# Four whole-unit buffers for the normalized attention output, and an earlier place for the chain of unit 3

## The chip, the cores and the metric

The kernel runs on one core of a Trainium2 chip. What counts is the device time of one launch, in microseconds. Three runs of the kernel before took 279.30, 278.63 and 280.29 us, a median of 279.3. The profiled execution of it took 279.81 us.

A core has five engines that run side by side and wait for each other through semaphores: PE (TensorE, matrix products into PSUM), DVE (VectorE), ACT (ScalarE), POOL (GpSimd) and SP (SyncE). POOL issues the loads here, SP issues the stores and the transposing DMAs.

## The reference

```
q, k, v: (8, 8, 576, 64)            # batch, heads, sequence, head_dim
per batch and head, in 9 chunks of 64 rows:
    attn = softmax(q_c @ k_c.T / 8)
    out  = attn @ v_c
x = out, heads side by side: (4608 tokens, 512)
h = x @ w_in                         # (512, 2048)
g = h * sigmoid(beta * h)            # beta: one value for each of the 2048 columns
result = g @ w_out                   # (2048, 512) -> (4608, 512), float32
```

## The kernel before

The 4608 tokens are cut into 18 units of 256 tokens. Two units make a block of 512, so there are 9 blocks, numbered j = 0 to 8. All products run in float16 with float32 sums in PSUM.

**Attention of a unit u** is a chain over four engines.

- `emit_T(u)` brings q and k into the layout that PE needs: two transposes on DVE (L161) for units below 9, two transposing DMAs on SP (L156) from unit 9 on. At its end `loads_to(u + 4)` lets POOL issue the loads of a later unit (L103, L109, L117). The q and k tiles have 4 buffers, so a load waits for the transpose of the unit four before.
- `emit_sc(u)` computes the scores on PE (L229, or L216 from unit 9 on) and their exponential on ACT (`et`, L238 or L222). With `split=True` the exponential is done in two halves.
- `emit_pv(u)` multiplies with v on PE (L267, or L253 from unit 8 on). v has an extra column of constant value, so that the row sum comes out beside the result.
- `emit_norm(u, s)` divides half s of the unit (128 tokens) by the row sum and writes `x16` in float16: a reciprocal (L302) and a product (L306) on DVE. From unit 8 on, `emit_norm_whole` does this with two reciprocals (L285, L287), two products on DVE (L275) and two small ones on ACT (L286).
- The transposed tile `xt` comes from `x16` in one of three ways: `emit_xt_pe(u, s)` by PE (L322) and a copy on ACT (L326); `emit_xt_unit(2)` the same for both halves at once (L334, L337); `emit_xt_dma(u, s)` by a transposing DMA on SP (L341), from unit 6 on.

The tiles `x16` come from the pool `x_p`. Units 0 to 7 take one tile of 1 KB per partition for each half, tag `x16`, 4 buffers. Units 8 to 17 take one tile of 2 KB for the whole unit, tag `x32`, 2 buffers. A buffer is free again when the PE transposes or the DMAs that read it are done.

**The first layer of a block**: `emit_m(j, m, c0, n)` computes 128 of the 2048 hidden columns, for n tokens (512, or 256 when a unit comes alone), with four matmuls (L365) into `hps`; ACT applies a tanh (`sg`, L377); DVE makes the gated value `gt` (`emit_mg`, L353). With `gate=False` the gate is not issued there but by a later `emit_mg`.

**The second layer.** For block 0 `emit_t(0, t, k0, k1)` multiplies row group t with rows k0 to k1 of w_out, four matmuls of 128x512 in a call (L390), into the PSUM tile `ops` of that row group. There are 16 calls: s = 0 to 3 outside, t = 0 to 3 inside. The last call for each t also copies the tile on ACT (L400) and stores it from SP (L402). The other blocks use seven products of smaller matrices in place of eight (`emit_prod`, L582), with sums of gates (`emit_sum`, L429) and differences of weights (`emit_wt`, L420).

**PSUM.** `hps`, `ops`, `xp` of `emit_xt_pe`, and the accumulators of block 1 share one pool with 4 buffers (`ps_p`, tag "p"). From unit 8 on, `emit_pv` takes two buffers of that pool (`xe`) beside its own tile in `ps_s`; the scores of the next unit take that same tile's place in `ps_s`.

**Order.** The order on every engine is the order in which the program emits the instructions (`tc.manual_schedule()`). Up to and with the first half of block 1 it is written out by hand. From there on a list of items with due times is sorted for each block; an item that is due earlier is emitted earlier. The hand-written part that matters is the second layer of block 0, with the attention of units 2 and 3 between its calls, and then the first eight `emit_m(1, ...)` on unit 2 alone, with the end of the chain of unit 3 between them:

```
sc(3)  m0 m1 m2(gate later)  pv(3)  norm(3,0) gate2  m3(gate later)  norm(3,1) gate3
m4  xt_pe(3,0)  m5  m6  xt_pe(3,1)  m7
```

After these come `emit_m(1, 0..7)` on the tokens of unit 3, from the sorted list.

Of the kernel before, what the change touches and what calls it, by code (L numbers as in the profile page):

```python
# [9 lines left out]
FP16 = mybir.dt.float16  # L10
# [5 lines left out]
def kernel(  # L16
# [11 lines left out]
    B, H, S, D = q.shape  # L28
# [4 lines left out]
    KFF = DFF // 128  # L33
# [112 lines left out]
    qT = {}  # L146
    kT = {}
# [131 lines left out]
    def emit_norm_whole(u, s):  # L279
        x, y = x_t[u][0:2]  # L280
        if s == 0:
            rx = rd_p.tile([128, 2, 8, 1], FP32, tag="rx", name="rx")
            x16 = x_p.tile([128, 2, 2, 4, D], FP16, tag="x32", name="x16", bufs=2)
            for r in range(2):
                nc.vector.reciprocal(out=rx[:, r, 7], in_=y[r][:, D:D + 1])  # L285
                nc.scalar.activation(out=x16[:, 1, r, 3], in_=y[r][:, 0:D], func=ACTF.Copy, scale=rx[:, r, 7])  # L286
            nc.vector.reciprocal(out=rx[:, :, 0:7], in_=x[:, :, :, D:D + 1])  # L287
            norm_part(x16[:, 0], x[:, :, 0:4], rx[:, :, 0:4])
            x_t[u] = (x, rx, x16)
            x16_t[u, 0] = x16[:, 0]  # L290
            return
        x, rx, x16 = x_t.pop(u)
        norm_part(x16[:, 1, :, 0:3], x[:, :, 4:7], rx[:, :, 4:7])
        x16_t[u, 1] = x16[:, 1]

    def emit_norm(u, s):
        if u >= WV:
            emit_norm_whole(u, s)
            return
        x = x_t.pop((u, s))  # L300
        rd = rd_p.tile([128, 2, 4, 1], FP32, tag="rd", name="rd")
        nc.vector.reciprocal(out=rd, in_=x[:, :, :, D:D + 1])  # L302
        x16 = x_p.tile([128, 2, 4, D], FP16, tag="x16", name="x16")
        for r in ([0, 1] if u < 2 else [slice(0, 2)]):
            o = x16[:, r]
            nc.vector.tensor_tensor(  # L306
                out=o, in0=x[:, r, :, 0:D], in1=rd[:, r].to_broadcast(list(o.shape)), op=ALU.mult
            )
        x16_t[u, s] = x16
# [101 lines left out]
    def emit_wt(i, qs=(0, 1)):  # L411
        for q in qs:
            o = [t[:, 4 * q:4 * q + 4, :] for t in wt]
            a, b = {
                0: (w_half(0, q, 1), w_half(0, q, 0)),
                1: (w_half(1, q, 1), o[0]),
                2: (w_half(1, q, 1), w_half(0, q, 1)),
                3: (w_half(1, q, 0), o[1]),
            }[i]
            nc.vector.tensor_tensor(out=o[i], in0=a, in1=b, op=ALU.subtract)  # L420
# [10 lines left out]
    def emit_beta():  # L431

        nc.vector.tensor_tensor(out=rb, in0=bt, in1=bt, op=ALU.mult)
        nc.vector.tensor_scalar(out=rb, in0=rb, scalar1=1e-20, scalar2=None, op0=ALU.is_lt)
        nc.vector.scalar_tensor_tensor(out=rb, in0=rb, scalar=2e-10, in1=bt, op0=ALU.mult, op1=ALU.add)
        nc.vector.tensor_scalar(out=bs, in0=rb, scalar1=2.0, scalar2=None, op0=ALU.mult)
        nc.vector.reciprocal(out=rb, in_=rb)
# [173 lines left out]
    with tc.manual_schedule():  # L611
# [62 lines left out]
            emit_m(0, m)  # L674
        for s in range(4):
            for t in range(4):
                if s == 2 and t == 1:
                    emit_T(2)
                    for i in (0, 2, 1, 3):
                        emit_wt(i, (0,))  # L680
                    emit_wt(0, (1,))
                if s == 2 and t == 2:
                    emit_sc(2)
                if s == 3 and t == 0:
                    emit_pv(2)
                    emit_norm(2, 0)
                    emit_norm(2, 1)
                    emit_T(3)
                if s == 3 and t == 3:
                    emit_xt_unit(2)  # L690
                emit_t(0, t, 4 * s, 4 * s + 4)
        emit_beta()
        emit_sc(3, True)
        for m in range(2):
            emit_m(1, m, 0, 256)
        emit_m(1, 2, 0, 256, gate=False)
        emit_pv(3)
        emit_norm(3, 0)
        emit_mg(1, 2)
        emit_m(1, 3, 0, 256, gate=False)  # L700
        emit_norm(3, 1)
        emit_mg(1, 3)
        emit_m(1, 4, 0, 256)
        emit_xt_pe(3, 0)
        emit_m(1, 5, 0, 256)
        emit_m(1, 6, 0, 256)
        emit_xt_pe(3, 1)
        emit_m(1, 7, 0, 256)

        def att_items(u, a0, w):  # L710
# [19 lines left out]
        for j in range(1, NB):  # L730
# [12 lines left out]
            items = []  # L743
            if j == 1:
                items += [(0.04 * m, 0, ("h", m)) for m in range(8)]
                items += [(0.32 + 0.085 * (m - 8), 0, ("m", m)) for m in range(8, KFF)]
                items += [(0.30, 3, ("T", 4)), (0.52, 2, ("sc", 4)), (0.70, 2, ("pv", 4)), (0.71, 3, ("norm", 4, 0)),
                          (0.80, 3, ("norm", 4, 1)), (0.56, 3, ("Th", 5, "kT")), (0.63, 3, ("Th", 5, "qT"))]
                items += [(c, 3, ("wt", i)) for i, c in ((1, 0.47),)]
            else:  # L750
                m0 = {2: 0.36, 4: 0.09}.get(j, 0.02)
                if j < QB:
                    items += [(m0 + (1 - m0) * m / KFF, 0, ("m", m)) for m in range(KFF)]
                else:
                    lane = LANE[2 if j == QB else j == NB - 1]
                    cost = [1 if it[0] == "q" and it[2] == 3 else 2 for it in lane]
                    for n, it in enumerate(lane):
                        c, e, f = (0.98 * sum(cost[:n + d]) / sum(cost) for d in (0, 1, 2))
                        items.append((c, 0, it))
                        if it[0] == "m":  # L760
                            items.append((c + 0.04, 3, ("mg", it[1])))
                        elif it[0] == "last":
                            pass
                        elif it[2] == 2:
                            if j == NB - 1 and it[1] == 3:
                                f = e
                            items += [(f - 0.002, 2, ("qs", it[1], 2)), (f - 0.001, 2, ("qs", it[1], 1)),
                                      (f + 0.03, 3, ("qt", it[1], 0))]
                        elif it[2] == 3:
                            items += [(c + 0.001, 2, ("qs", it[1], 0)), (c + 0.04, 3, ("qt", it[1], 1))]  # L770
                    if j == QB:
                        items.append((0.18, 6, ("open",)))
                        items += [(0.20 + 0.01 * n, 6, ("tx", QB, n)) for n in range(4)]
                        items += [(0.26 + 0.01 * n, 6, ("ws", 2, n)) for n in range(4)]
                        items += [(0.40 + 0.02 * n, 5, ("ws", 3, n)) for n in range(4)]
                        items += [(0.62 + 0.02 * n, 5, ("ws", 1, n)) for n in range(4)]
                    if j + 1 < NB:
                        items += [(0.70 + 0.06 * n, 5, ("tx", j + 1, n)) for n in range(4)]
                for i, p in enumerate((1, 2, 6, 5, 7, 3, 4)):
                    for t in range(2):  # L780
                        w = 1.06 if j == NB - 1 else 0.98
                        items.append(((0.002 if j >= QB else 0) + w * (2 * i + t) / 14, 1, ("prod", p, t)))
                if j == NB - 1:
                    for i, c in ((2, 0.72), (0, 0.80), (1, 0.86)):
                        items.append((c, 4, ("pre", i)))
                for i in range(4):
                    s0 = (0.01, 0.08, 0.25, 0.33)[i] if j == 2 else 0.005 + 0.07 * i
                    if j >= QB:
                        s0 = (0.003, 0.10, 0.33, 0.48)[i]
                    items.append((s0, 4, ("sum", i)))  # L790
                if j == 2:
                    items += [(c, 3, ("wt", i)) for i, c in ((2, 0.36), (3, 0.55))]
                    items += [(0.03, 0, ("sc", 5)), (0.06, 2, ("xp", 4, 0)), (0.09, 2, ("xp", 4, 1)),
                              (0.17, 2, ("pv", 5)), (0.18, 3, ("norm", 5, 0)), (0.19, 3, ("norm", 5, 1)),
                              (0.24, 3, ("T", 6)), (0.53, 3, ("T", 7)), (0.60, 3, ("T", 8)), (0.61, 3, ("T", 9)), (0.80, 3, ("T", 10)),
                              (0.30, 2, ("xp", 5, 0)), (0.32, 2, ("xp", 5, 1))]
                for u, a0, w in ATT.get(j, ()):
                    items += att_items(u, a0, w)
# [87 lines left out]
```

## Time and profile before

| | |
|---|---|
| median of three runs | 279.3 us (278.63 to 280.29) |
| profiled execution: whole time, span of its instructions | 279.81 us, 277.9 us |
| DVE busy | 208.8 us, 75% of the span |
| ACT busy | 165.1 us, 59% |
| POOL busy | 95.4 us, 34% |
| granted TensorE clock | 0.9 or more of full speed in all 40 slices |
| DMA | 36.42 MB, 131 GB/s in the mean; 0.9 busy or more in each of the first 27 of 40 slices |
| transposing DMA of `xt`, issue to landing | 2.4 to 9.0 us, median 6.4 (24 of them) |
| load of a whole unit's k (128 KB), issue to landing | median 11.8 us |

The profile tells for each engine when it was busy, and for each idle stretch which event ended it. "Busy" on PE is modelled and overlaps from one matmul to the next, so the time that a group takes is read from its start to the start of the next group. In a row of a timeline the first number is the start in us from the start of the span, the second the duration, then engine, line, operation, the tiles that are written and read, the shape and the count; in brackets the idle time of the engine before it and what ended it. A row of the list of waits names the waiting engine and line, then what it waited for, then the total, the number of times and the longest, in us.

### The profile page before, as it was taken

The page shows a single profiled execution, that of the slowest core. Times are in us where ns is not written, and L with a number is a line of the kernel's source. Part 1 is how long each engine was busy: PE and PEld are TensorE (multiplying, and loading weights), DVE is VectorE, ACT ScalarE, POOL GpSimd, SP SyncE. Part 2 cuts the span into 40 slices and gives each one's busy share as a digit, 9 for nine tenths or more (in the row PEclk, how much of TensorE's full clock was granted, in tenths as well). Part 3 has the DMA queues.
Part 4 walks back from the last instruction along what each step waited for, and adds up shares of the span by engine and source line. Part 5 has one row for each costly group of instructions (what it writes and reads, how often), then busy time and mean ns, then how long its engine had stood idle before and what let it go on. Part 6 is the DMA issues. An engine that isn't in the chain of part 4 may idle for free.

```text
span 277.9 us, 7779 instructions
## 1 busy us (share of the span) xinstructions
PE 268.0 (96%) x3226; PEld 183.7 (66%) x3226; DVE 208.8 (75%) x391; ACT 165.1 (59%) x295; POOL 95.4 (34%) x122
## 2 busy tenths in 40 slices
PE   8799999899999999999999989999999999999995
PEld 3565446656756566666666656666877887788874
DVE  2567566899988688668865857679997978787961
ACT  3378416886555566556555744667557495858721
POOL 8954478498539843343336310000000000000000
PEclk9999999999999999999999999999999999999999
DMA  9999999999999999999999999973112102110223
GB/s 138 163 195 203 190 180 187 233 173 167 171 130 132 169 166 153 177 142 140 154 150 194 140 155 212 186 133 88 38 41 75 40 0 78 38 40 0 77 78 113
DMA packets 141762, 36.42 MB, mean 131 GB/s; under 512 B 125856, under 2 KB 141216, under 8 KB 141728
## 3 DMA queue, kind: packets, MB, share of 16 engines
q0 software_dynamic: 99136, 18.10, 84.4%
q1 hardware_dynamic: 42592, 17.84, 34.9%
q8 instruction: 25, 0.41, 0.6%
q14 instruction: 9, 0.07, 0.1%
HBM read 36.71 MB, written 9.44 MB: 166 GB/s over the span
## 4 chain that ended last, share of the span: by engine, by line
PE 65%; DVE 13%; DMA 10%; ACT 6%; issue 3%; POOL 2%; SPq 0%; ACTq 0%; DVEq 0%; POOLq 0%
PE hps L365 24%; PE ya L582 12%; PE yb L582 9%; DMA xt<-x 5%; PE acc L582 5%; PE ops L390 4%; PE qx L478 3%; DMA qu<-in_q_dram 3%; ACT hq L510 3%; PE qz L478 3%; DVE gt L353 3%; DVE gt L524 2%; DMA h<-in_k_dram 2%; DVE x L306 2%; PE sc L229 1%
## 5 line engine op out<-in xcount | busy, mean ns | idle before, releaser
L365 PE MATMUL hps<-xt,win 128*128 128x512 f16 (+1 forms) x504 | 110.8, 356 | 1.7 <-ACT xt L326 0.7
L353 DVE SCALAR_TENSOR_TENSOR gt<-sg,hps 128x512 f16<-128x512 f32 (+1 forms) x113 | 68.8, 617 | 32.4 <-ACT sg L377 31.5
L377 ACT ACTIVATE sg<-hps,bt 128x512 f32<-128x512 f32 (+1 forms) x113 | 70.5, 636 | 36.8 <-PE hps L365 36.4
L365 PEld LDWEIGHTS <-win 128*128 128x128 f16 x504 | 47.7, 98 | 35.3 <-issue 2.5
L582 PEld LDWEIGHTS <-sm 128*128 128x128 f16 x512 | 49.4, 98 | 12.5 <-issue 0.3
L582 PEld LDWEIGHTS <-gt 128*128 128x128 f16 x384 | 36.8, 98 | 10.4 <-DVE gt L524 0.6
L117 POOL DMA_DIRECT2D vbig<-in_v_dram x40 | 33.8, 854 | 24.9 <-DMA ku<-in_k_dram 6.3
L582 PE MATMUL ya<-wt,sm 128*128 128x256 f16 x200 | 25.9, 273 | 0.0
L103 POOL DMA_DIRECT2D qu<-in_q_dram x20 | 17.0, 855 | 16.7 <-DVE qT L161 7.1
L103 POOL DMA_DIRECT2D ku<-in_k_dram x20 | 16.9, 857 | 14.7 <-DMA qu<-in_q_dram 7.6
L524 DVE TENSOR_SCALAR gt<-hq,rb 128x512 f16<-128x512 f32 x32 | 14.5, 482 | 7.5 <-ACT hq L510 6.5
L429 DVE TENSOR_TENSOR sm<-gt 128x2048 f16<-128x2048 f16 (+1 forms) x17 | 19.7, 1156 | 0.3
L510 ACT ACTIVATE hq<-hq,bs 128x256 f32<-128x256 f32 (+1 forms) x32 | 17.1, 610 | 1.8 <-DVE hq L503 1.8
L238 ACT ACTIVATE et<-sc 128x1024 f16<-128x1024 f32 (+1 forms) x10 | 8.3, 852 | 12.3 <-PE sc L229 12.3
L275 DVE TENSOR_TENSOR x<-x,rx 128x512 f16<-128x512 f32 (+1 forms) x20 | 11.9, 620 | 4.4 <-DMA xt<-x 4.2
L599 ACT COPY osb<-ya 128x512 f32<-128x512 f32 x18 | 10.6, 589 | 7.6 <-PE ya L582 7.1
L390 PE MATMUL ops<-wout,gt 128*128 128x512 f16 x64 | 14.5, 379 | 0.0
L582 PE MATMUL yb<-wout,gt 128*128 128x256 f16 x104 | 13.9, 273 | 0.2
L478 PEld LDWEIGHTS <-ws 128*128 128x128 f16 x128 | 12.5, 98 | 2.0 <-issue 0.6
L582 PE MATMUL yb<-wt,sm 128*128 128x256 f16 x104 | 13.5, 273 | 0.1
L582 PE MATMUL ya<-wout,gt 128*128 128x256 f16 x104 | 13.5, 273 | 0.0
L582 PE MATMUL yb<-wout,sm 128*128 128x256 f16 x104 | 13.5, 273 | 0.0
(99 smaller groups left out, 347.0 us busy)
## 6 DMA issues: line engine op xcount, KB each, us to landing
out_dram<-osb SPq DMA_DIRECT2D x32, 256.0 KB, 3.5
vbig<-in_v_dram POOLq DMA_DIRECT2D x32, 128.0 KB, 7.2
qu<-in_q_dram POOLq DMA_DIRECT2D x18, 128.0 KB, 7.8
ku<-in_k_dram POOLq DMA_DIRECT2D x18, 128.0 KB, 11.8
win<-in_moe_w_in_dram POOLq DMA_DIRECT2D x8, 256.0 KB, 9.1
wout<-in_moe_w_out_dram POOLq DMA_DIRECT2D x4, 512.0 KB, 12.8
qu<-in_q_dram POOLq DMA_DIRECT2D x5, 256.0 KB, 6.6
ku<-in_k_dram POOLq DMA_DIRECT2D x5, 256.0 KB, 7.2
```

The lines of the kernel that those rows point to most:

```text
L103: nc.gpsimd.dma_start(out=tv[off:off + n, sp], in_=src[b, :, s:s + n, :].rearrange("h p d -> p h d"),)
L117: nc.gpsimd.dma_start(out=vbig[off:off + n, i % NV, :, 0:D], in_=v[b, :, s:s + n, :].rearrange("h p d -> p h d"),)
L275: nc.vector.tensor_tensor(out=x16, in0=x[:, :, :, 0:D], in1=rd.to_broadcast(list(x16.shape)), op=ALU.mult)
L353: nc.vector.scalar_tensor_tensor(out=gt_t[j][:, m, c0:c0 + n], in0=sg[:, 0:n], scalar=1.0, in1=hps[:, 0:n], op0=ALU.add, op1=ALU.mult,)
L365: nc.tensor.matmul(out=hps[:, 0:n], lhsT=w_in16[m // 2][:, kk, (m % 2) * 128:(m % 2) * 128 + 128], rhs=xr[:, c0 // CH:(c0 + n) // CH, 2 * ...
L377: nc.scalar.activation(out=sg[:, 0:n], in_=hps[:, 0:n], func=ACTF.Tanh, scale=bt[:, m:m + 1])
L390: nc.tensor.matmul(out=ops, lhsT=gt_t[j][:, kk, t * 128:(t + 1) * 128], rhs=w_out16[kk // 4][:, kk % 4, :], start=(kk == 0), stop=(kk == K ...
L429: nc.vector.tensor_tensor(out=sm[i][:, lo:hi, :], in0=a, in1=b, op=op)
L478: nc.tensor.matmul(out=dst[:, s, :], lhsT=lhsT, rhs=rhs, start=(p in (1, 2, 5) and s == 0 and kk == 0), stop=(s == 1 and kk == 1), skip_gr ...
L510: nc.scalar.activation(out=o, in_=src, func=ACTF.Silu, scale=bs[:, m:m + 1])
L524: nc.vector.tensor_scalar(out=gt_t[j][:, m, :], in0=hq[:, b].rearrange("p c q -> p (c q)"), scalar1=rb[:, m:m + 1], scalar2=None, op0=ALU. ...
L582: nc.tensor.matmul(out=dst, lhsT=lhsT, rhs=rhs, start=(p in (1, 2, 5) and kk == 0 and (t == 0 or last)), stop=(kk == 7 and (t == 1 or last ...
```

## The change

Two things are changed, in the tile pool and in the hand-written order; no instruction is added or removed.

First, all units take whole-unit tiles `x16` of 2 KB from one tag with the pool's 4 buffers. Units below 8 allocate the tile in `emit_norm(u, 0)` and write its halves. The pool takes the same 8 KB per partition.

Second, in the second layer of block 0 the attention of units 2 and 3 is emitted one call of `emit_t` earlier, and the last call, `emit_t(0, 3, 12, 16)`, is emitted after pv(3). `emit_beta` comes before `emit_T(2)`. T(3) does q before k. The second half of the weight difference `wt[0]` comes after T(3). In the first eight `emit_m(1, ...)`, m 0 and 1 (in place of 2 and 3) have their gates issued later, m 2 has it behind those of m 0 and 1, and `emit_xt_pe(3, 1)` stands before m 6.

```
         if s == 0:
             rx = rd_p.tile([128, 2, 8, 1], FP32, tag="rx", name="rx")
-            x16 = x_p.tile([128, 2, 2, 4, D], FP16, tag="x32", name="x16", bufs=2)
+            x16 = x_p.tile([128, 2, 2, 4, D], FP16, name="x16")
...
+    xw_t = {}
+
     def emit_norm(u, s):
...
-        x16 = x_p.tile([128, 2, 4, D], FP16, tag="x16", name="x16")
+        if s == 0:
+            xw_t[u] = x_p.tile([128, 2, 2, 4, D], FP16, name="x16")
+        x16 = xw_t[u][:, s]
...
         for s in range(4):
             for t in range(4):
-                if s == 2 and t == 1:
+                if s == 2 and t == 0:
+                    emit_beta()
                     emit_T(2)
                     for i in (0, 2, 1, 3):
                         emit_wt(i, (0,))
-                    emit_wt(0, (1,))
-                if s == 2 and t == 2:
+                if s == 2 and t == 1:
                     emit_sc(2)
-                if s == 3 and t == 0:
+                if s == 2 and t == 3:
                     emit_pv(2)
                     emit_norm(2, 0)
                     emit_norm(2, 1)
-                    emit_T(3)
-                if s == 3 and t == 3:
+                    emit_T(3, ("qT", "kT"))
+                    emit_wt(0, (1,))
+                if s == 3 and t == 2:
                     emit_xt_unit(2)
-                emit_t(0, t, 4 * s, 4 * s + 4)
-        emit_beta()
+                if s < 3 or t < 3:
+                    emit_t(0, t, 4 * s, 4 * s + 4)
         emit_sc(3, True)
-        for m in range(2):
-            emit_m(1, m, 0, 256)
-        emit_m(1, 2, 0, 256, gate=False)
+        emit_m(1, 0, 0, 256, gate=False)
+        emit_m(1, 1, 0, 256, gate=False)
         emit_pv(3)
         emit_norm(3, 0)
+        emit_mg(1, 0)
+        emit_t(0, 3, 12, 16)
+        emit_m(1, 2, 0, 256, gate=False)
+        emit_norm(3, 1)
+        emit_mg(1, 1)
         emit_mg(1, 2)
-        emit_m(1, 3, 0, 256, gate=False)
-        emit_norm(3, 1)
-        emit_mg(1, 3)
+        emit_m(1, 3, 0, 256)
         emit_m(1, 4, 0, 256)
         emit_xt_pe(3, 0)
         emit_m(1, 5, 0, 256)
+        emit_xt_pe(3, 1)
         emit_m(1, 6, 0, 256)
-        emit_xt_pe(3, 1)
         emit_m(1, 7, 0, 256)
```

A third edit writes the constant 0.085 as 0.0850 and changes nothing.

More of the change, by code (lines that the diff above doesn't have):

```diff
@@ L745 @@
                 items += [(0.04 * m, 0, ("h", m)) for m in range(8)]
-                items += [(0.32 + 0.085 * (m - 8), 0, ("m", m)) for m in range(8, KFF)]
+                items += [(0.32 + 0.0850 * (m - 8), 0, ("m", m)) for m in range(8, KFF)]
                 items += [(0.30, 3, ("T", 4)), (0.52, 2, ("sc", 4)), (0.70, 2, ("pv", 4)), (0.71, 3, ("norm", 4, 0)),
```

## The prediction

> **What bounds the kernel now.** I read the page's busy times first, then the list of who waited for whom on PE, then the timeline of PE, DVE and ACT around each wait.
>
> ```profile
> PE 268.0 (96%) x3226; PEld 183.7 (66%) x3226; DVE 208.8 (75%) x391; ACT 165.1 (59%) x295; POOL 95.4 (34%) x122
> ```
>
> PE is the bound: about 10 us of the 277.9 us span are not PE, and some 6 of those are the head and the tail. So a gain can only be PE time that is a wait. The list for PE (total, times, longest) has the few that matter here:
>
> ```profile
> PE hps L365 <- ACT xt L326: 0.7, 3, 0.3
> PE hps L365 <- ACT x L286: 0.6, 1, 0.6
> PE xp L322 <- DVE x L306: 0.5, 1, 0.5
> PE sc L216 <- PE hps L365: 0.4, 1, 0.4
> ```
>
> The first and third belong to the chain of unit 3, at 46 to 53 us; the second and fourth to the normalization of unit 14, at 162 to 166 us. PE's timeline of the first place (start, duration, work):
>
> ```profile
> 46.29 0.71 PE L229 MATMUL sc<-qT,kT 32*64 32x64 f16 x64
> 46.94 1.48 PE L365 MATMUL hps<-xt,win 128*128 128x256 f16 x12
> 48.35 0.45 PE L267 MATMUL x<-vbig,et 64*64 64x65 f16 x32
> 48.73 1.05 PE L365 MATMUL hps<-xt,win 128*128 128x256 f16 x8
> 50.24 0.40 PE L322 MATMUL xp<-ident,x 128*128 128x128 f16 x4 [0.46 <-DVE x L306]
> 50.56 0.60 PE L365 MATMUL hps<-xt,win 128*128 128x256 f16 x4
> 51.31 0.60 PE L365 MATMUL hps<-xt,win 128*128 128x256 f16 x4 [0.15 <-ACT xt L326]
> 51.74 0.39 PE L322 MATMUL xp<-ident,x 128*128 128x128 f16 x4
> 52.06 0.60 PE L365 MATMUL hps<-xt,win 128*128 128x256 f16 x4
> 52.94 6.24 PE L365 MATMUL hps<-xt,win 128*128 128x256 f16 x44 [0.28 <-ACT xt L326]
> ```
>
> Durations overlap, so I count from start to start. Twelve 256-wide matmuls take 48.35 - 46.94 = 1.41 us with a 0.11 us change of shape, so one m (four of them) is 0.43. Then 48.73 to 50.24 is 1.51 for two m (0.87): 0.64 lost. 50.56 to 51.31 is 0.75 for one: 0.32 lost. 52.06 to 52.94 is 0.88 for one: 0.45 lost. Together 1.4 us. Why the transpose at 50.24 was late is in DVE's and ACT's timelines:
>
> ```profile
> 48.55 0.78 DVE L353 SCALAR_TENSOR_TENSOR gt<-sg,hps 128x256 f16<-128x256 f32 x2 [1.31 <-ACT sg L377]
> 49.25 0.20 DVE L302 RECIPROCAL rd<-x 128x8 f32<-128x8 f32 x1
> 49.49 0.69 DVE L306 TENSOR_TENSOR x<-x,rd 128x512 f16<-128x512 f32 x1
> ```
> ```profile
> 47.07 1.09 ACT L238 ACTIVATE et<-sc 128x512 f16<-128x512 f32 x2
> ```
>
> The gates of m 0 and 1 stand before the normalization on DVE, and they waited for ACT, which did the exponentials until 48.16. The second place (all engines, cut to its rows):
>
> ```profile
> 161.70 1.04 PE L582 MATMUL yb<-wout,gt 128*128 128x256 f16 x8
> 162.94 0.52 ACT L286 ACTIVATE x<-xe,rx 128x64 f16<-128x64 f32 x2 [3.43 <-DMA xt<-x]
> 162.95 0.69 DVE L275 TENSOR_TENSOR x<-x,rx 128x512 f16<-128x512 f32 x1 [2.44 <-DMA xt<-x]
> 163.30 1.02 PE L365 MATMUL hps<-xt,win 128*128 128x512 f16 x4 [0.56 <-ACT x L286]
> ```
>
> Unit 14 takes the buffer of unit 12 (two buffers), whose transposing DMA was issued by SP only at 155.67 and landed at 162.83 in the chain of waits. ACT and DVE stand still, a PSUM bank stays taken, and PE runs out: 161.70 to 163.30 is 1.60 for 0.87 of work, 0.73 lost. The next scores (165.03 to 166.46) need the bank that DVE releases with its second product at 165.81: 1.43 for 0.87 and a usual 0.1, so 0.46 lost. Together 1.2 us.
>
> **The four buffers.** No instruction is added: the same products write into halves of one tile. Unit 14 now takes unit 10's buffer, whose DMA was issued at 131.61 and, at the longest landing of this kind (9.0 us), was done by 141. ACT's turn then is right after its reciprocal (160.29 + 0.23), and PE wants the bank at 162.57: 2 us of cover. The waits of units 13 and 15 go too, but PE felt neither. Gain: 1.2 us; bounds 0.7 (only the first gap closes) and 1.2 (both).
>
> **The chain of unit 3.** One group (four 128x512, 8.73 us for ten groups between 30.71 and 39.44, so 0.87) moves from before the scores to behind the PV product, so sc(3) starts at 46.29 - 0.87 = 45.42, and sc(2) at 38.57, pv(2) at 41.04. What each needs:
> - T(2) still waits for the load of ku (35.77) and ends at 37.08: 1.5 us before sc(2), where 2.4 were.
> - norm(2) moves with pv(2) and ends at 43.2. T(3) follows, q first: qT 43.1, kT 43.7 to 44.4. POOL's wait that ended at 43.07 on a ku landing tells that unit 3's k is in by 43.0: 0.7 us before kT and 1.7 before it would hold sc(3).
> - beta's five DVE operations (45.20 to 47.24) go before T(2), where DVE sat idle 3.45 us; the subtraction wt(0), 0.6 us, goes behind T(3), where DVE has nothing until the reciprocal at 47.4. Both cost nothing; without that cover 2.0 and 0.6 us of DVE.
> - The store of the last row group leaves SP about 2 us later; the next store on SP is at 71.83. POOL's loads for unit 7 wait for T(3), but also for a DMA lane until 57.37: unmoved.
>
> A sentence apart: the Trainium skill, "SBUF — State Buffer", on the shared port pair, says that a VectorE operation with two SBUF inputs can shut GpSimd's reads out for its whole length, and by that (an estimate, if issuing reads through it) the moved subtraction could hold POOL's loads for up to 0.65 us; the time would stay 277.2, since the loads it would meet, of unit 5, are not used before 61 us. Here POOL issued two loads in 1.40 us at 37.51 while such subtractions ran, no slower than its mean of 0.85 for one.
>
> Now the walk, by the durations above. m 0 and 1 from 46.07; ACT's exponentials end at 48.16 - 0.87 = 47.29, so the second half of pv(3), due at 47.24, waits about 0.1. The kept group runs 47.55 to 48.42, m 2 to 48.85. DVE meanwhile does reciprocal 47.43 (0.38 after the product's start, as at 41.91 and 42.29), product 47.67 to 48.36, gate 0 to 48.68, the second half to 49.53, gate 1 to 49.86, gate 2 to 50.26. m 3 takes m 0's bank: 48.85, on time. m 4 takes the kept group's bank, which ACT has copied at 48.42 + 0.2 + 0.59 = 49.2: on time at 49.28. The transpose of half 0 takes m 1's bank: 49.9, 0.2 late. m 5 needs gate 2: 50.3. Half 1 at 50.73, m 6 at 51.08 (ACT's xt copy ends at 51.03), m 7 to 51.94, and the next m needs the second xt copy: 52.0 against 52.94. Gain 0.9 us. Bounds: 1.4 if every loss goes; below nothing, -0.4, if DVE's and ACT's queues, now with one PSUM bank less for a while, stop PE twice more by 0.64, the longest stop of this stretch. I take the walk.
>
> Another sentence apart: the Trainium skill, "TensorE: Matmul & The Clock Gate", on a second failure mode, says that short idles between groups from cycling PSUM banks can make the clock drop to half; by it the 5 us of matmuls in this stretch, which with one bank held idles in just this way, could take twice as long, and the sum would be about 282 us (an estimate from that page). Here the granted clock is 1.00 from 45 to 60 us with those very idles in it.
>
> **Sum.** 0.9 + 1.2 = 2.1 us: the span goes to 275.8. The profiled run took 279.81, 1.9 us beyond its span and 0.5 over the median of 279.3; off the median that is **277.2 us**. What is earlier on PE must not be late on a DMA. Closest is the first m of block 3 at 98.16: its xt came from a DMA issued at 90.67, and by the median landing of 6.4 it was in at 97.1. PE would want it at 97.3, and its DMA is issued 0.9 earlier as well. Scores of unit 16 (176.1) have their transposed q, issued until 165.75, by about 171.5.
>
> **Rivals.**
> - *Only one part pays.* Loads keep DMA busy in nearly every tenth up to 190 us, and transposes land after 2.4 to 9.0 us. If the landing of block 3 stays or slips by 0.9, the first gain is handed back at 98 us, and 1.2 stays: 278.1. If instead the chain gains and the 162 us wait returns as another wait there, 0.9 stays: 278.4. For: the narrow 0.2 us at 97. Against: PE never waited for a DMA in this trace.
> - *Slower: unit 3's k comes late.* T(3) sits one group earlier, in DVE's strict order, before the wt subtraction and norm(3). From a landing at 44.7 on, PE loses each microsecond, at 46.8 both gains are gone, and at 48.2 the kernel is slower by over 0.5%. A ku issued at 34.91 with the median landing of its kind (11.8) comes at 46.7, and with 13.8 (the median of the q loads of 64 KB) at 48.7: 277.2 + 4.0 = 281.2. Against: it came by 43.0 here, and the loads ahead of it don't move.
> - *It does more.* All 1.4 goes in the chain and the 0.42 us before the scores at 65.86 as well: 276.3.
>
> **Chances.** The forecast 0.68 (its own range 276.4 to 278.0), one part 0.20, slower 0.07, more 0.05. The three runs before spread over 0.6%, so about 0.5%, 1.4 us, is what a measurement can tell from no change; that line is at 277.9. Faster: 0.9 of the first, all of the last and a quarter of the second, 0.71, cut to 0.68 for the margin of only 0.7 us; same 0.25; slower 0.07. Range: 276.3 (the third rival) to 278.9 (one part, with 0.5 of scatter).
>
> **What would show it.** PE's timeline between sc(3) and the next block of m's: 6.6 us with the kept group in it (6.65 without, before); no 0.46 idle ahead of the first xp; sc(3) near 45.4. No wait of ACT L286 or L275 on DMA xt, and m after m at 162 us without a gap. It is wrong if kT for unit 3 waits for ku, if the m's after pv(3) wait 0.5 us or more on gates, or if an hps near 97 us waits for xt.

## The result and the profile after

The kernel after takes 278.08 us (median of 9 runs, 277.3 to 278.34) and the kernel before 279.3 us (9 runs, 278.63 to 280.29): a ratio of 0.9953, 95% interval [0.9936, 0.9971], or 1.3 us less (0.8 to 1.8; the medians differ by 1.2). The interval does not reach 1, so the kernel is faster, but by just under the half per cent that the prediction drew as its line. A second measurement gave 0.9946 [0.9932, 0.996]. The forecast was 2.1 us less. The profiled execution of after took 278.0 us with a span of 276.2.

The page's busy line of after first (busy us, share of the span, instructions):

```profile
PE 268.1 (97%) x3226; PEld 184.2 (67%) x3226; DVE 208.5 (75%) x391; ACT 165.0 (60%) x295; POOL 95.4 (35%) x122
```

PE's work is what it was, 268 us in 3226 instructions; the span lost idle time only. PE's timeline of after from sc(3) on (start, duration, work):

```profile
45.78 0.71 PE L229 MATMUL sc<-qT,kT 32*64 32x64 f16 x64
46.43 1.05 PE L369 MATMUL hps<-xt,win 128*128 128x256 f16 x8
47.40 0.83 PE L267 MATMUL x<-vbig,et 64*64 64x65 f16 x32
48.17 1.04 PE L394 MATMUL ops<-wout,gt 128*128 128x512 f16 x4
49.04 1.47 PE L369 MATMUL hps<-xt,win 128*128 128x256 f16 x12
50.35 0.39 PE L326 MATMUL xp<-ident,x 128*128 128x128 f16 x4
50.71 0.60 PE L369 MATMUL hps<-xt,win 128*128 128x256 f16 x4
51.14 0.39 PE L326 MATMUL xp<-ident,x 128*128 128x128 f16 x4
51.55 4.74 PE L369 MATMUL hps<-xt,win 128*128 128x256 f16 x41
```

No bracket of idle time is left: the waits of 0.46, 0.15 and 0.28 us of before are gone, and the kept group (48.17) stands in the same 6.6 us. The one stop is inside the PV product: 47.40 to 48.17 is 0.77 us for what took 0.38 before. DVE in after (the transposes of unit 3, then the first rows of the normalization):

```profile
35.95 0.71 DVE L161 STREAM_TRANSPOSE kT<-ku 128x512 f32<-128x512 f32 x1 [2.12 <-DMA ku<-in_k_dram]
...
43.47 0.72 DVE L161 STREAM_TRANSPOSE qT<-qu 128x512 f32<-128x512 f32 x1
44.09 0.67 DVE L161 STREAM_TRANSPOSE kT<-ku 128x512 f32<-128x512 f32 x1
...
47.80 0.21 DVE L304 RECIPROCAL rd<-x 128x8 f32<-128x8 f32 x1 [2.47 <-PE x L267]
48.05 0.69 DVE L310 TENSOR_TENSOR x<-x,rd 128x512 f16<-128x512 f32 x1
48.66 0.41 DVE L357 SCALAR_TENSOR_TENSOR gt<-sg,hps 128x256 f16<-128x256 f32 x1
```

kT of unit 2 waits for its load, as before; q and k of unit 3 (43.47, 44.09) wait for nothing. The reciprocal comes as soon as the product gives it something, and the gate stands behind it. Unit 14 in after, in the timelines of ACT, DVE and PE:

```profile
159.84 0.52 ACT L286 ACTIVATE x<-xe,rx 128x64 f16<-128x64 f32 x2 [0.83 <-DVE rx L285]
...
160.05 0.69 DVE L275 TENSOR_TENSOR x<-x,rx 128x512 f16<-128x512 f32 x1
...
161.20 1.04 PE L586 MATMUL yb<-wout,gt 128*128 128x256 f16 x8
162.07 1.03 PE L369 MATMUL hps<-xt,win 128*128 128x512 f16 x4
162.94 1.04 PE L586 MATMUL ya<-wt,sm 128*128 128x256 f16 x8
163.81 1.03 PE L369 MATMUL hps<-xt,win 128*128 128x512 f16 x4
164.77 0.45 PE L216 MATMUL sc<-qT,kT 64*64 64x64 f16 x32
```

ACT and DVE go on when the reciprocal is there, not when a DMA lands, and PE's blocks follow each other at 0.87 us. The second gap of before, ahead of the scores, is closed as well: there these two rows stood 1.43 us apart, and in after the same two (163.81 and 164.77) stand 0.96 apart.

```profile
165.03 1.03 PE L365 MATMUL hps<-xt,win 128*128 128x512 f16 x4
166.46 0.45 PE L216 MATMUL sc<-qT,kT 64*64 64x64 f16 x32 [0.40 <-PE hps L365]
```

**Where the time went, in one table.** All kernels issue the same 3226 matmuls, so an instruction can be counted out in each trace. "Start" is when the first second-layer matmul begins, ahead of every instruction that the new order moves. "Chain" is from there to the 151st first-layer matmul (56.21 us in the profile of before), and "unit 14" from the 641st to the 705th of the score matmuls that read qT and kT (L216 and L229; 145.99 to 166.46 in before). Between and behind these stretches every profile takes 89.8 and 111.4 to 111.5 us, but for the one marked. The last column is the idle time of DVE's first product of unit 14 (L275) that ended with the landing of an xt DMA. All in us.

| profile | start | chain | unit 14 | span | DVE waits for xt |
|---|---|---|---|---|---|
| before | 30.71 | 25.50 | 20.47 | 277.9 | 2.44 |
| before, second | 31.21 | 25.50 | 19.75 | 277.7 | 1.72 |
| before, third | 31.00 | 25.50 | 19.63 | 277.4 | 1.60 |
| before, fourth | 31.63 | 25.50 | 20.57 | 278.9 | 2.53 |
| buffers only | 30.97 | 25.50 | 19.28 | 277.0 | none |
| buffers only, second | 30.77 | 25.49 | 19.28 | 276.8 | none |
| order only | 30.93 | 24.65 | 19.34 | 276.1 | 1.30 |
| order only, second | 31.08 | 24.46 | 19.28 | 276.1 | 0.92 |
| after | 31.06 | 24.64 | 19.28 | 276.2 | none |
| after, second | 30.71 | 24.58 | 19.28 | 275.8 | none |
| three buffers | 31.24 | 24.57 | 19.29 | 276.3 | none |
| gates first | 31.76 | 24.73 | 19.29 | 277.0 | none |
| no kept group | 30.66 | 25.33 | 19.29 | 276.5 | none |
| later scores (90.2 between) | 30.96 | 24.50 | 19.29 | 276.4 | none |

### The profile page after: what moved, and what is told of

It is laid out like the page before. It is cut to its first block, busy times and chain, and to the rows that moved or that the text cites. A ratio compares the mean times of both kernels' runs of the same rounds, so it can differ in the third digit from the quotient of the medians.

```text
span 276.2 us, 7795 instructions
## 1 busy us (share of the span) xinstructions
PE 268.1 (97%) x3226; PEld 184.2 (67%) x3226; DVE 208.5 (75%) x391; ACT 165.0 (60%) x295; POOL 95.4 (35%) x122
## 4 chain that ended last, share of the span: by engine, by line
PE 73%; DVE 10%; DMA 6%; ACT 5%; POOL 3%; issue 2%; DVEq 0%; ACTq 0%; POOLq 0%
PE hps L369 27%; PE ya L586 13%; PE yb L586 10%; PE acc L586 5%; PE ops L394 5%; PE qx L482 3%; DMA qu<-in_q_dram 3%; ACT hq L514 3%; PE qz L482 3%; DMA win<-in_moe_w_in_dram 3%; DVE gt L528 2%; DVE gt L357 2%; PE sc L229 1%; DVE sm L433 1%; POOL vbig L117 1%
## 5 line engine op out<-in xcount | busy, mean ns | idle before, releaser
L378 ACT ACTIVATE sg<-hps,bs 128x512 f32<-128x512 f32 x13 | 8.8, 687 | 7.2 <-PE hps L369 7.2
```

## Experiments

The theories: **A**, both gains are steady, 0.9 and 1.2 us, and what is missing is scatter; **B**, the loss at unit 14 varies from run to run, because it ends with the landing of a DMA, and the first profile of before caught a long one; **C**, the gain of the chain is given back at unit 14 when the buffers stay two, since the DMA's landing stays where it is.

**Each part alone, and both kernels again.** For the buffers alone:

```diff
-            x16 = x_p.tile([128, 2, 2, 4, D], FP16, tag="x32", name="x16", bufs=2)
+            x16 = x_p.tile([128, 2, 2, 4, D], FP16, name="x16")
...
-        x16 = x_p.tile([128, 2, 4, D], FP16, tag="x16", name="x16")
+        if s == 0:
+            xw_t[u] = x_p.tile([128, 2, 2, 4, D], FP16, name="x16")
+        x16 = xw_t[u][:, s]
```

For the order alone, the rest of the change, and these lines as they were.

- Before, unchanged. Expected: 

> The kernel before, unchanged, for the spread between executions and for a second profile of it. Theory A (both gains are steady, 0.9 and 1.2 us, and the first 20 us of an execution vary by some 0.4 us with the landing of the first loads): ratio 1.000 within its interval; the loss at the unit-14 normalization is again 1.1 to 1.2 us and the loss in the chain of unit 3 again 1.4 us, while the first m of unit 1 on PE starts anywhere within 0.4 us of the first profile. Theory B (the profiled execution of before had a worse wait than usual at unit 14, since that wait ends with a DMA): the loss there is now 0.6 us or less, and the rest is as it was.


 Measured: 279.58 us, ratio 1.001 [0.9998, 1.0021].
- Buffers only. Expected: 

> Only the four whole-unit buffers; the hand-written order is that of before. Theory A: 1.2 us faster, ratio 0.996, and no wait of ACT L286 or DVE L275 on the DMA of xt; the chain of unit 3 still loses 1.4 us. Theory B: 0.3 to 0.6 us faster, ratio 0.998 to 0.999, with the same picture in the profile.


 Measured: 278.84 us, ratio 0.9989 [0.9973, 1.0004].
- Order only. Expected: 

> Only the hand-written order of the change; the tiles of normalized x as before (two whole-unit buffers from unit 8 on). Theory A with the transposing DMAs moving along with PE: 0.9 us faster, ratio 0.997, and the wait at unit 14 is as long as before (1.2 us). Theory C (the DMA that frees the buffer lands at a fixed time): the chain wins 0.9 us at 53 us and gives it back at 162 us, where the loss grows from 1.2 to about 2.1 us; ratio 0.999 to 1.000.


 Measured: 277.88 us, ratio 0.9954 [0.9941, 0.9967].
- After, unchanged. Expected: 

> The changed kernel, unchanged, in the same comparison as the two halves and the kernel before. Theory A: ratio 0.9925 to 0.9955; the two halves add up to it. Its profile repeats the 6.6 us from the scores of unit 3 to the next block of m and has no gap at unit 14; the start of the first m of unit 1 varies by some 0.4 us.


 Measured: 277.6 us, ratio 0.9946 [0.9932, 0.996].

The order alone brings nearly all of it, 1.3 us (0.9 to 1.6), and the buffers alone 0.3 us with an interval that takes in nothing. So A is wrong for the buffers. C is refuted by the unit-14 column: with two buffers and the new order PE loses 0.06 us there, not 2.1. A had expected 1.2 there and is wrong on this as well. With the new order, SP's stream of DMAs came earlier too. The second transposing DMA of unit 12 was issued at 155.67 in the first profile of before, at 155.05 in the second, and at 153.52 with the order only; DVE's first product could go on at 162.95, 162.72 and 161.18. Counted from each profile's own start, and with the profiles of the next section, this issue stands at 123.8 to 125.0 us in the four of before and at 122.6 and 121.4 in the two of the order only. From it to the product it is 7.3 to 7.7 us in the four of before, and 7.7 and 8.3 in the two, so the issue carries most of the difference. That the order alone moves it by more than PE's 0.9 is not shown: with the buffers alone, in the old order, it stood at 122.2 in one profile and 124.1 in the other.

**More profiles of before and of the order alone, and the buffers again.** To settle B, the size of the loss was read in two more profiles of before. The kernels are those above, with no further edit.

- Expected of the third profile of before: 

> The kernel before, unchanged: a third profile of it, for the size of PE's loss at unit 14 alone, which was 1.2 us in the first profile and about 0.6 in the second. Theory B (the loss varies from run to run, because the wait ends with the landing of a transposing DMA, and the first profile caught a long one): below 1.0 us here, anything from 0 to 0.9. Theory A (it is a steady 1.2 us): 1.1 to 1.3.


- Expected of the fourth: 

> The kernel before, unchanged: a fourth profile. As for the third: theory B 0 to 0.9 us lost by PE between 160 and 167 us, theory A 1.1 to 1.3.


- Order only, second profile. Expected: 

> The new order with the buffers of before (four halves, two whole units), as already measured: a second profile. In the first, ACT's multiply of unit 14 still waited 1.3 us on the landing of unit 12's transposing DMA, and PE lost nothing. If the earlier order takes this wait off PE for good: again a wait below 1.6 us and no loss on PE. If that was chance: a wait of 2 us or more and a loss of 0.4 to 1.2.


- Buffers only, again. Expected: 

> Four whole-unit buffers in the order of before, as already measured at a ratio of 0.9989 [0.9973, 1.0004]. Theory A (1.2 us): 0.9957. Theory B (the mean loss of before is 0.3 to 0.6 us): 0.998 to 0.999. No wait of ACT L286 or DVE L275 on a DMA of xt in either.

The two profiled runs of before took 279.3 and 280.84 us, that of the order only 277.96. The buffers alone took 278.96 us, ratio 0.9998 [0.9982, 1.0013], less of a gain than the 0.998 to 0.999 that B expected, though its interval takes that in. DVE's first product of unit 14 in the third profile of before:

```profile
162.40 0.69 DVE L275 TENSOR_TENSOR x<-x,rx 128x512 f16<-128x512 f32 x1 [1.60 <-DMA xt<-x]
```

in the fourth:

```profile
163.96 0.69 DVE L275 TENSOR_TENSOR x<-x,rx 128x512 f16<-128x512 f32 x1 [2.53 <-DMA xt<-x]
```

and in the second profile of the order only:

```profile
160.75 0.69 DVE L275 TENSOR_TENSOR x<-x,rx 128x512 f16<-128x512 f32 x1 [0.92 <-DMA xt<-x]
```

Put beside the unit-14 column these give a plain rule. Without any wait the stretch takes 19.28 us. The waits of 2.44, 1.72, 1.60, 2.53, 1.30 and 0.92 us came with losses of 1.19, 0.47, 0.35, 1.29, 0.06 and 0.00: the loss is the wait less 1.25 us, and never below nothing. 1.25 us is the cover that PE has here. B holds: the loss is the small difference of two longer times, and a wait that is 0.93 us longer takes it from 0.35 to 1.29. The fourth profile missed what B expected of it (0 to 0.9): by itself it would have spoken for A, and the third for B. Only the four together show that the loss varies. The second profile of the order only came out as expected of a loss that is gone for good: a wait below 1.6 us and nothing lost.

**Three buffers instead of four** (in the new order):

```diff
-            x16 = x_p.tile([128, 2, 2, 4, D], FP16, name="x16")
+            x16 = x_p.tile([128, 2, 2, 4, D], FP16, tag="x16", name="x16", bufs=3)
...
-            xw_t[u] = x_p.tile([128, 2, 2, 4, D], FP16, name="x16")
+            xw_t[u] = x_p.tile([128, 2, 2, 4, D], FP16, tag="x16", name="x16", bufs=3)
```

Expected: 

> The kernel after, with three whole-unit buffers in place of four. With three, unit 14 takes the buffer of unit 11, whose second transposing DMA landed at 151.08 us in the trace of after, some 9 us before unit 14 asks for it. Theory A (each buffer beyond two that is free in time is worth its whole wait, and no more): the same as after, 277.6 to 278.1, no wait of ACT L286 or DVE L275 on a DMA of xt. Rival (the fourth buffer does something of its own, for instance for the halves of units 2 to 5 that now share the tag): a wait appears somewhere before 100 us and the time stands 0.3 us or more above after.

Measured: 277.84 us, ratio 0.9943 [0.9923, 0.9963]; no wait of ACT L286 or DVE L275 on an xt DMA. The fourth buffer does nothing.

**The order of the gates, and the kept group**, each undone alone. Gates first:

```diff
-        emit_m(1, 0, 0, 256, gate=False)
-        emit_m(1, 1, 0, 256, gate=False)
+        emit_m(1, 0, 0, 256)
+        emit_m(1, 1, 0, 256)
         emit_pv(3)
         emit_norm(3, 0)
-        emit_mg(1, 0)
         emit_t(0, 3, 12, 16)
         emit_m(1, 2, 0, 256, gate=False)
         emit_norm(3, 1)
-        emit_mg(1, 1)
         emit_mg(1, 2)
```

Expected: 

> The kernel after, but the gates of m 0 and 1 of block 1 stand again before the normalization of unit 3 on DVE; the kept group stays behind the PV product. Theory G (the order of the gates is what the 0.9 us comes from): gates 0 and 1 wait for ACT's tanh until about 48.4 us, the first reciprocal slips from 47.8 to 48.6, the first transpose comes 0.5 us late or more, and the time is 0.4 to 0.9 us above after. Theory K (the kept group is what it comes from, since it gives PE 0.87 us of work while ACT and DVE catch up, and gates that come early also free their banks early): PE loses at most 0.2 us and the time is that of after within 0.3.

No kept group:

```diff
-                if s < 3 or t < 3:
-                    emit_t(0, t, 4 * s, 4 * s + 4)
+                emit_t(0, t, 4 * s, 4 * s + 4)
...
         emit_mg(1, 0)
-        emit_t(0, 3, 12, 16)
```

Expected: 

> The kernel after, but no group is kept back: all four groups of the last row group stand before the scores of unit 3, so the gates have the new order and nothing fills PE behind the PV product. Theory K: sc(3) is back near 46.6, and the 0.87 us that the group filled comes back as idle time of PE ahead of m 3, of the first transpose and of the m's after it: 0.6 to 1.0 us above after. Theory G: the new order of the gates alone brings most of the 0.9 us, and the time stands 0 to 0.4 above after.

Gates first: 277.96 us, ratio 0.9944 [0.9916, 0.9972]; the chain takes 24.73, 0.1 more than after. No kept group: 278.52 us, ratio 0.9976 [0.9962, 0.9989]; the chain takes 25.33, 0.7 more. DVE and then PE with the gates first:

```profile
48.73 0.79 DVE L357 SCALAR_TENSOR_TENSOR gt<-sg,hps 128x256 f16<-128x256 f32 x2 [2.70 <-ACT sg L381]
```
```profile
50.83 0.39 PE L326 MATMUL xp<-ident,x 128*128 128x128 f16 x4
51.58 0.60 PE L369 MATMUL hps<-xt,win 128*128 128x256 f16 x4 [0.37 <-DVE gt L357]
```

The gates again hold up DVE until ACT's tanh is there, but the transpose at 50.83 no longer feels it, because the kept group ahead of it gave DVE the time; what is left is one m that waits 0.37 us. The 0.39 us that this costs from start to start came back for the most part in other rows: the PV product took 0.55 in place of 0.77, and the second transpose and what stood between it and the next m 0.22 in place of 0.41. The first of these is no merit of the gates alone: the same product took 0.80 and 0.59 us in the two profiles of the order only. By the times there is no difference (ratio 0.9944, and 0.9943 for three buffers in the same measurement).

PE without a kept group:

```profile
48.41 1.77 PE L369 MATMUL hps<-xt,win 128*128 128x256 f16 x12
50.75 0.38 PE L326 MATMUL xp<-ident,x 128*128 128x128 f16 x4 [0.57 <-DVE gt L357]
51.08 0.60 PE L369 MATMUL hps<-xt,win 128*128 128x256 f16 x4
```

From the first of these three m's to the transpose after was 1.31 us; here it is 2.34, of which 0.57 stands by name against a gate. So theory K: the 0.87 us of work put behind the product is what most of the gain of the chain is made of (0.7 of 0.9), and the order of the gates, with that work in place, is worth 0.1 at most, which is no more than the chain differs between profiles of one order (24.46 and 24.65 for the order only).

**A further move**, at the second largest wait left between 20 and 100 us:

```diff
-                    items += [(c, 3, ("wt", i)) for i, c in ((2, 0.36), (3, 0.55))]
-                    items += [(0.03, 0, ("sc", 5)), (0.06, 2, ("xp", 4, 0)), (0.09, 2, ("xp", 4, 1)),
+                    items += [(c, 3, ("wt", i)) for i, c in ((2, 0.36), (3, 0.47))]
+                    items += [(0.075, 0, ("sc", 5)), (0.06, 2, ("xp", 4, 0)), (0.09, 2, ("xp", 4, 1)),
```

Expected: 

> The kernel after, and two more moves: the scores of unit 5 stand one product later (0.075 in place of 0.03 of block 2), and the last weight subtraction earlier (0.47 in place of 0.55). The scores waited 0.26 us by name on the second product of unit 4's normalization at 65.34 us, about 0.4 from start to start; the product ahead of them fills that. If the stall is only covered, 0.3 to 0.4 us below after, 277.2 to 277.7; if the later scores make the exponentials or the PV product of unit 5 late, the same as after or 0.3 above. The subtraction is expected to bring 0 to 0.4 at 90.8 us, where an m waits 0.34 for a gate.

Measured: 278.19 us, ratio 0.9961 [0.9949, 0.9974]; no better than after. PE in its trace:

```profile
64.69 0.39 PE L326 MATMUL xp<-ident,x 128*128 128x128 f16 x4
...
65.88 0.71 PE L229 MATMUL sc<-qT,kT 32*64 32x64 f16 x64
...
70.51 0.40 PE L326 MATMUL xp<-ident,x 128*128 128x128 f16 x4 [0.25 <-DVE x L310]
```

The scores no longer wait, but everything of unit 5 behind them comes later on DVE, and at 70.51 a transpose waits for the second product of its normalization, 0.42 us from start to start, as much as was taken away. Further on, an m at 81.15 waits 0.16 us for a gate. The m that waited 0.34 for a gate at 90.80 waits 0.34 at 90.94: the earlier subtraction brought nothing. From the end of the chain to unit 13 this kernel takes 90.2 us and the others 89.8.

## Why the prediction was right, and which term was mis-sized

- **Direction and mechanism** were right: faster, no new wait, unit 3's k in time, the wait at unit 14 gone. 278.08 and the second 277.6 lie within 276.3 to 278.9, 0.9 and 0.4 above the 277.2. The first is just outside the narrower 276.4 to 278.0 that the forecast itself was given, and above the 277.9 drawn there as the line of a gain that a measurement can tell; the second is within both.
- **Chain of unit 3, 0.9 us: right.** 25.50 became 24.46 to 24.65 in every kernel with the whole new order, 0.85 to 1.04 less. sc(3) came at 45.78, and at 45.43 in the second profile of after, which has the start of the first profile of before (30.71): 45.4 was forecast. The walk's remainder was right as a sum and not in its parts: the PV product took 0.39 longer than before, where 0.1 was reckoned, and the transpose that was to be 0.2 late waits for nothing by name. PE came to the product 1.62 us after sc(3), as by the walk (47.43 - 0.38 - 45.42 = 1.63), and its second half began 0.29 us after the first half's start, where it was 0.15 in before, close to the 0.1 reckoned for ACT's exponentials. The rest is a stop inside the second half, 0.28 us from its first to its ninth matmul where before had 0.07. The profile names nothing that ended it, and its cause is open; it was 0.31 and 0.11 in the two profiles of the order only.
- **Four buffers, 1.2 us with bounds 0.7 to 1.2: the term that was mis-sized.** Both bounds were read from one execution, and they say how much of its two gaps closes, not how much the gaps differ from run to run. In four profiles they are 1.19, 0.47, 0.35 and 1.29; by the times, the buffers alone are worth 0.3 us in one measurement and 0.06 in the other. A second reckoning: the stretches that do not vary, with unit 14 at its 19.28, sum to 246.0 us in before, the start of the 14 profiles is 31.05 in the mean, and the median span of the timed runs of before is 277.3 to 277.5 where it was the kernel compared with and 277.7 in its own twelve runs; that leaves 0.2 to 0.6 for the loss, if these runs start like the profiled ones. Why the profiled executions show a mean of 0.8 stays open: four are few.
- **The sum, 0.9 + 1.2: not a sum.** The two parts share the loss. In both profiles of the order only SP's issue comes up as well, by more than PE's 0.9, so the wait falls to about the 1.25 us of cover (1.30 and 0.92) and the buffers find almost nothing left to do. The unit-14 column shows this; the times alone would not, since 0.3 and 1.3 add up to the 1.5 of both within their intervals. The prediction did see that the DMA would be issued 0.9 earlier in block 3, and did not carry this to unit 14. Order only should give 0.9 and the 0.2 to 0.6: 1.1 to 1.5, measured 1.3. Both together the same and some 0.1 outside the span (below): measured 1.3 and 1.5.
- **The base.** The sum was taken off the median, while the profile that gave the terms stood 0.5 above it. The long wait of 1.19 us was part of what made that execution slow, although it had nearly the earliest start of all. Off its own 279.81 the sum gave 277.7, and the profiled run of after took 278.0: right within 0.3, which is the 0.35 by which its start is later. Term and base have to be of one execution.
- **The rivals.** "Only one part pays" named 278.1 for a landing of block 3 that is late, and the time is 278.08, but not by that way: the m at 97.66 in after waits for nothing. What happened is its kin, one part pays since the other has little to win. "k comes late": no wait (DVE's lines above). "It does more": the stop before the scores of unit 5 is still there, 0.26 by name, and moving it moved the loss.
- **The two rules of the Trainium skill.** By "TensorE: Matmul & The Clock Gate", on a second failure mode, short idles between groups could have halved the clock in this stretch. It did not happen here: in after and in the kernel without a kept group, where PE idles 0.57 us for a gate, the granted clock is 1.00 from 45 to 55 us. By "SBUF — State Buffer", on the shared port pair, the moved subtraction could have held POOL up, if issuing a load reads through that port. It did not: it ran from 44.69 to 45.34 us in after, nearly all of it beside POOL's issue of a q load (44.44 to 45.31), which took 0.87 us, and 0.88 in before.

## What to carry to other kernels

A wait that ends with a DMA is the difference of two long times; before it is counted as a gain, its spread is read from several profiles, and its cover (how long a wait PE doesn't feel, here 1.25 us) from the pairs of wait and loss. Two edits that both take their gain from one wait are not summed, and an edit that moves the main engine up can move the queues that feed it too. Work kept in hand behind a chain of small steps, 0.87 us here, did more than a better order of those steps.

## What the runs showed that was not expected

- The first 31 us, ahead of everything that the new order moves, vary by 1.1 us from profile to profile (30.66 to 31.76; 30.71 to 31.63 in the four of before), nearly as much as the change is worth. In the fourth profile of before an m at 14.32 us waited 0.58 us for the load of win and a PV product at 15.96 0.34 for ACT; in the first profile neither did.
- Runs with the whole-unit buffers take 1.77 to 1.80 us beyond their span in the mean of each measurement, those with the two old tags 1.89 to 1.91. So 0.1 us of the gain is outside the span. Why is open.
- SP's issue of a transposing DMA is long and not constant: for one and the same q it took 3.82 us (150.33 to 154.15) and 3.90 in the first and fourth profiles of before, 2.98 and 3.00 in the second and third. The two profiles with the longer issue are those with the longer wait at unit 14.
